# Sums of w2 in a fused attention and FFN kernel: places of their own in the first half's chunks, GpSimd additions beside the queries

## The chip, the cores and the metric

The kernel runs on one core of a Trainium2 chip. The metric is the device time in microseconds (us) of one execution; lower is better. In the text TensorE is the engine that the profile calls PE (PEld its weight loads), VectorE is DVE, ScalarE is ACT, GpSimd is POOL, and SP is the engine that issues most DMAs.

## The reference

One block: layer norm, linear attention with 32 heads of 18, and a gated FFN, on 2048 rows of 576 features, all in float32.

```python
phi = lambda t: jnp.where(t > 0, t + 1, jnp.exp(t)) + 1e-6
pq, pk = phi(q), phi(k)
kv = jnp.einsum("bhsd,bhse->bhde", pk, v);  z = jnp.einsum("bhsd->bhd", pk)
o = einsum("bhqd,bhde->bhqe", pq, kv) / (einsum("bhqd,bhd->bhq", pq, z) + 1e-6)
s = merge_heads(o) @ wo
h = gelu(xn @ w1 + b1)          # 4608 columns
g = silu(h @ w2 + b2)
out = x + s * g
```

## The kernel before

**Arithmetic.** Every product is made of float32r matmuls: each operand is split into a high part (a cast on ScalarE, `hi`) and a low part (a subtraction, mostly on VectorE, `lo`), and three products of parts are added. Around that stands a Strassen scheme: a 2x2 block product takes seven products, numbered 1 to 7, whose operands 4 to 7 are sums and differences of blocks. So w1, w2 and the activations need sums before they are split. For w2 these sums are blocks added to blocks. The function `add_to` makes such a sum with a DMA that accumulates into its destination; GpSimd issues it (line 497 in the profile), and may wait for one before issuing the next.

**Stages.** (1) Keys, values and the state, in pairs of row tiles. (2) Query rounds r = 0 to 9, one pair of tiles each (the class `Proj` for the projection, `Attend` for the attention product with kw = state x wo). A round has 14 steps; steps 0 to 6 stand behind the seven products of the projection (in the order 1, 6, 7, 5, 2, 4, 3; their PSUM banks are a, b, z, e), steps 7 to 12 beside the two attention products (ps_s) and the transposes of the next pair's scaled queries (ptp, source pbuf, split into th and tl). Beside the queries, w2's sums 5 and 6 for chunks 4 to 8 are formed, split (w2o) and stored to DRAM. (3) The FFN in two halves of the rows, each going through nine chunks of w2. A chunk has 28 steps: 14 behind the products of two up blocks (`Up`, banks a, b, zy, e), then 14 behind the two halves of the seven down products (`product`, pm, in the order 1, 2, 7, 4, 5, 3, 6), whose results VectorE adds to macc. Steps 7 to 15 form the activations' sums (`HOps.S`, GpSimd), and their splits are h_h and h_l. In the first half, each chunk also loads the next chunk's w2, forms its sums 7 and 4, and forms and splits the next w1 blocks (`W1.T` on GpSimd, tiles w1t and w1raw; `hi` and `lo` give wa, wb, w).

**What sets the order.** The whole order is written by hand: `add(step, function, ...)` appends to a table, and `at_step(step)` issues what stands there once TensorE's part of the step has been issued. Each engine works through its instructions strictly in that order, so one that waits holds everything behind it. `plan_w1` puts the work on a w1 block into the table by two tables of steps, P1 (the second block of a chunk) and P0 (the first block of the next chunk).

**Sums 7 and 4 of a chunk.** Product 7's operand is B(0,1) + the block at (1,1); it is accumulated into the raw tile w2raw. Product 4's has a tile of its own, w2t4: it is loaded, the block (1,0) is accumulated into it, and at last the finished sum 7 (`sum4`, part 1). The tile pool `fr` also has the tags w2t5 and w2t6, which only the tail uses.

Of the kernel before, what the change touches and what calls it, by code (L numbers as in the profile page):

```python
# [8 lines left out]
F32 = mybir.dt.float32  # L9
# [6 lines left out]
P = 128  # L16
S = 2048
D = 576
HD = 288
# [7 lines left out]
CF = 4  # L27
NC = NF // CF
# [9 lines left out]
NSP = 14  # L38
# [4 lines left out]
def linear_attention_gated_ffn(ctx, tc, x, wqkv, wo, w1, b1, w2, b2, out):  # L43
    nc = tc.nc
    SUB, MUL, ADD = ALU.subtract, ALU.mult, ALU.add
# [426 lines left out]
    w2raw, w2op = {}, {}  # L472

    def w2_blocks(c):
        return w2[c].rearrange("p (r n a d) -> p r n a d", r=2, n=2, a=2)
# [15 lines left out]
    def w2_block(c, i):  # L491

        r, n = {5: (0, 0), 6: (1, 1), 4: (1, 0)}[i]
        return w2raw[c][r][:, n]

    def add_to(dst, src):
        nc.gpsimd.dma_start(dst, src, accum_op=ADD)

    def w2_sum(j):
        c, i = SUMS[j]  # L500
        add_to(w2_block(c, i), {5: w2_blocks(c)[:, 0, 1], 6: w2_block(c, 5), 4: w2_block(c, 6)}[i])

    def w2_hi(j):
# [13 lines left out]
    def add(step, fn, *args):  # L517
        plans.setdefault(step, []).append((fn, args))
# [195 lines left out]
    for p in range(1, NPAIR):  # L714
        plan_pair(p)
        base = p * NSP
# [36 lines left out]
    base = NPAIR * NSP  # L753
# [23 lines left out]
    kw_h = kwp.tile([P, KT, D], F32R, name="kw_h")  # L777
    kw_l = kwp.tile([P, KT, D], F32R, name="kw_l")
# [4 lines left out]

    krs = []

    def split_kw(k, elo):
        nc.scalar.copy(kw_h[:, k, :], krs[k])
        elo.tensor_tensor(kw_l[:, k, :], krs[k], kw_h[:, k, :].bitcast(F32), op=SUB)

    def fold_wo(hooks):  # L790

# [199 lines left out]
    for r in range(NPAIR + 2):  # L991
        base = (NPAIR + r) * NSP
        if r <= 5:
            for k, i in enumerate(RELOAD[r]):
                add(base + (9, 11, 12)[k], x_reload, i)
        if r < NPAIR:
            a, b = q_tiles(r)
        if 2 <= r <= NPAIR:
            late = 2 * (r == 2)
            add(base + late, den_mul, r - 1, 1)  # L1000
            for s in range(2):
                add(base + 2 + s + late, den_sum, r - 1, s)
                add(base + 2 + s + late, den_div, r - 1, s)
        if 1 <= r < NPAIR:
            add(base + (12 if r > 1 else 15), den_mul, r, 0)
            add(base + (4 if r != 2 else 5), pad, 0)
            add(base + (6 if r != 2 else 7), pad, 1)
            if r > 1:
                add(base + 9, p_hi, r - 1, 0)
                add(base + 9, p_lo, r - 1, 0)  # L1010
            add(base + NSP, p_hi, r - 1, 1)
            add(base + NSP + 1, p_lo, r - 1, 1)
        if 1 <= r < NPAIR:
            a, b = q_tiles(r)
            at = base + 2 * (r == 2)
            add(at + 7, phi_exp, a, e_bufs[0])
            add(at + 7, phi_exp, b, e_bufs[1])
            add(at + 7, phi_max, a, e_bufs[0])
            add(at + 8, phi_max, b, e_bufs[1])
            add(at + (8 if r > 1 else 14), phi_add, a)  # L1020
            add(at + (9 if r > 1 else 15), phi_add, b)
        if r == 1:
            add(base + NSP + 2, split_kw, 2, nc.vector)
            add(base + NSP + 4, split_kw, 3, nc.vector)
        if 2 <= r <= 6:
            add(base, w2_load, r + 2, *((w1p, "wa") if r % 2 == 0 else (w2rp, "w2raw")))
        if r == 2:
            add(base + 8, w2_sum, 2 * r + 5)
        if 3 <= r <= 7:
            n = 2 * r + 3  # L1030
            add(base + 1, w2_sum, n + 1)
            if r < 7:
                add(base + 8, w2_sum, n + 2)
            for j in range(2):
                add(base + 7 + j, w2_hi, n + j)
                add(base + 9 + j, w2_lo, n + j)
        if r == 0:
            phi_exp(a, e_bufs[0]), phi_exp(b, e_bufs[1])
            fold_wo({
                0: [lambda: phi_max(a, e_bufs[0]), lambda: phi_max(b, e_bufs[1])],  # L1040
                1: [lambda: phi_add(a), lambda: phi_add(b), lambda: den_mul(0, 0), lambda: den_mul(0, 1)],
            })
            split_kw(0, nc.vector)
            den_all(0, 0)
            add(base + NSP + 2, den_all, 0, 1)
            add(base + NSP + 3, split_kw, 1, nc.vector)
        elif r < NPAIR:
            pr = Proj(Q_ORDER[r], wkq, q_tiles(r), mu2)
            for k, i in enumerate(K_UP):
                pr.step(i)  # L1050
                if (r, k) == (2, 0):
                    transpose_p(0, 1)
                if (r, k) == (1, 5):
                    transpose_p(0, 0), p_hi(0, 0), p_lo(0, 0)
                at_step(base + k)
        if 1 <= r < NPAIR:
            for s in range(2):
                at = Attend(r - 2, s) if r >= 2 else None
                for k in range(2):
                    if at:  # L1060
                        at.part(7 * k, 7 * k + 7)
                    at_step(base + 7 + 3 * s + k)
                if at:
                    at.store()
                    transpose_p(r - 1, s)
                at_step(base + 9 + 3 * s)
            if r == 7:
                w1t[0], w1t[1] = W1(0), W1(1)
                w2_raw0.append(load_w2_raw(0))
        if r == 0:  # L1070
            for k in range(9, 14):
                at_step(base + k)
        elif r == NPAIR:
            w = w1t[0]
# [12 lines left out]
            p_hi(r - 1, 0), p_lo(r - 1, 0)  # L1087
            pad(1)
            w.hi("a"), w.lo("a")
            w.T(4)  # L1090
            at.part(7, 14)
            at.store()
            transpose_p(r - 1, 1)
            p_hi(r - 1, 1), p_lo(r - 1, 1)
        elif r > NPAIR:
            for s in range(2):
                at = Attend(r - 2, s)
                at.part(0, 14)
                at.store()
                if s == 0:  # L1100
                    for j in (6, 7, 5):
                        w.hi(j), w.lo(j)
                else:
                    for j in ("b", 4):
                        w.hi(j), w.lo(j)
# [8 lines left out]
    fr = ctx.enter_context(tc.tile_pool(name="fr", bufs=1, side="right", reuse_waits="tile"))  # L1114
# [67 lines left out]
    class W2:  # L1182


        def __init__(self, n):
            self.n, self.ops, self.tiles = n, {}, {}

        def load_raw(self):
            self.raw = raw = load_w2_raw(self.n) if self.n else w2_raw0[0]
            self.B = lambda r, n: raw[:, r, n]  # L1190
            self.src = {1: self.B(0, 0), 2: self.B(1, 0), 3: self.B(1, 1), 7: self.B(0, 1)}
            if 0 < self.n < NC:
                self.src[4] = fr.tile([P, CF // 2, HD], F32, tag="w2t4", name=f"w2t4_{self.n}", bufs=1)
                nc.sync.dma_start(self.src[4], w2_blocks(self.n)[:, 0, 0])

        def sum7(self):
            add_to(self.src[7], w2_blocks(self.n)[:, 1, 1])
# [235 lines left out]
    def plan_w1(add, w, base, T, hi, lo):  # L1433
# [8 lines left out]
    )  # L1442
    P0 = dict(
        T={5: 24, 6: 24, 7: 25, 4: 25},
        hi={"a": 14, 6: 25, 7: 26, 5: 26, "b": 27, 4: 27},
        lo={"a": 14, 6: 25, 7: 26, 5: 26, "b": 27, 4: 27},
    )


# [19 lines left out]
    w2t = {}  # L1469
# [5 lines left out]
    for step in range(n_chunks):  # L1475
# [4 lines left out]
        if half == 0:  # L1480
            plan_w1(add, w1t[2 * step + 1], base, **P1)
            w2c = w2t[step]
            if not step:
                add(base + 2, w2c.sum7)
            for i, at in (PW2 if step else PW2_FIRST).items():
                add(base + at, w2c.hi, i)
                add(base + at, w2c.lo, i)
            if step == 0:
                for i, at in W2_SUMS_FIRST.items():
                    add(at, w2t[0].load, i)  # L1490
        if half == 0 and c < NC - 1:
# [2 lines left out]
            add(base + 13, lambda n=2 * step + 2: plan_w1(add, w1t[n], base, **P0))  # L1494
            make(W2, w2t, step + 1)
            nxt = w2t[step + 1]
            add(base + (8 if step else 10), nxt.load_raw)
            add(base + (16 if step else 17), nxt.sum7)
            add(base + (16 if step else 17), nxt.sum4, 0)
            add(base + 21, nxt.hi, 2)  # L1500
            add(base + 21, nxt.lo, 2)
            add(base + (21 if step else 22), nxt.sum4, 1)
            add(base + 27, nxt.hi, 4)
            add(base + 27, nxt.lo, 4)
            for i, at in W2_SUMS_NEXT.items():
# [103 lines left out]
```

## Time and profile before

| | us |
|---|---|
| median of 3 runs (1120.41 to 1122.63) | 1121.7 |
| the profiled execution | 1122.14 |
| its span, first to last instruction | 1120.4 |
| TensorE busy | 1098.9 |
| VectorE busy | 810.8 |
| ScalarE busy | 505.4 |
| GpSimd busy | 459.5 |
| mean granted TensorE clock | 0.996 |

An instruction's row has its start in the span, its duration, engine, line, operation and output<-inputs; in brackets stand the engine's idle time before it and what ended it. A row of waits has the total, the number and the longest. Buffer numbers are left out of most names, so several tiles can share one. The query rounds 2 to 7 lie between 180 and 275 us, the first half's chunks between 291 and 709.

### The profile page before, as it was taken

How to read it: one execution, taken by the hardware profiler on the slowest of the kernel's cores; microseconds unless marked ns; L12 is line 12 of the kernel's file. 1: busy time of each engine (PE TensorE's matmuls, PEld its weight loads, DVE VectorE, ACT ScalarE, POOL GpSimd, SP SyncE). 2: the span in 40 equal slices, each digit the busy share in tenths (PEclk: the TensorE clock that was granted, in tenths of full speed). 3: DMA queues.
4: the chain of work that ended last, by engine and by line, in shares of the span. 5: the costliest groups of instructions: out<-in, count | busy, mean ns of one | idle time of the engine just before them, and what ended most of it. 6: DMA issues, size and time to landing. Idle time of an engine off the chain costs nothing.

```text
span 1120.4 us, 18755 instructions
## 1 busy us (share of the span) xinstructions
PE 1098.9 (98%) x6924; PEld 1017.2 (91%) x6924; DVE 810.8 (72%) x1242; ACT 505.4 (45%) x913; POOL 459.5 (41%) x419
## 2 busy tenths in 40 slices
PE   8999999999999999999999999999999999999997
PEld 7899998999898998988989889899898998988987
DVE  6877666656598888988889888666475574664756
ACT  6766554535545454454544544524233242242352
POOL 5854433344354444544545434324224132242340
PEclk9999999999999999999999999999999999999999
DMA  5887747895998679687796879977666666766243
GB/s 202 299 265 275 257 129 216 275 293 197 349 313 336 198 267 316 190 333 225 246 320 180 318 208 373 369 263 261 216 200 225 206 203 210 230 198 223 87 135 120
DMA packets 95818, 272.50 MB, mean 243 GB/s; under 512 B 10413, under 2 KB 21165, under 8 KB 93679
## 3 DMA queue, kind: packets, MB, share of 16 engines
q1 hardware_dynamic: 89391, 258.32, 65.2%
q0 software_dynamic: 6336, 12.98, 7.4%
q8 instruction: 55, 0.90, 0.3%
q14 instruction: 36, 0.29, 0.1%
HBM read 165.05 MB, written 100.01 MB: 237 GB/s over the span
## 4 chain that ended last, share of the span: by engine, by line
PE 90%; DVE 4%; ACT 3%; DMA 1%; issue 1%; POOL 1%; DVEq 0%; POOLq 0%; ACTq 0%
PE pm L1279 32%; PE e L1141 12%; PE a L1141 10%; PE zy L1141 10%; PE ps_s L885 5%; PE pl L411 5%; PE b L1141 4%; PE e L356 2%; PE z L356 2%; PE a L356 2%; PE pd L1402 2%; DVE h_l L915 1%; PE ps_kva L464 1%; DMA kr<-kw 1%; PE b L356 1%
## 5 line engine op out<-in xcount | busy, mean ns | idle before, releaser
L912 ACT CAST h_h<-g 128x512 fp32r<-128x512 f32 x204 | 120.1, 621 | 140.6 <-PE pm L1279 139.5
L915 DVE TENSOR_TENSOR h_l<-g,h_h 128x512 fp32r<-128x512 f32 x204 | 169.3, 830 | 0.0
L1287 DVE TENSOR_TENSOR macc<-macc,pm 128x576 f32<-128x576 f32 x128 | 96.1, 751 | 36.8 <-PE pm L1279 36.7
L1246 POOL TENSOR_TENSOR mid<-g 128x512 f32<-128x512 f32 x34 | 44.0, 1294 | 184.7 <-ACT g L1149 184.7
L1141 PE MATMUL a<-xH,wa 128*128 128x512 f32 x360 | 117.1, 390 | 0.0
L1289 DVE TENSOR_TENSOR macc<-pm,macc 128x576 f32<-128x576 f32 x90 | 68.0, 755 | 18.4 <-PE pm L1279 17.6
L1149 ACT ACTIVATE g<-b,b1c 128x512 f32<-128x512 f32 x36 | 24.8, 688 | 124.5 <-DVE b L1167 124.5
L1141 PEld LDWEIGHTS a<-xH,wa 128*128 128x128 f32 x360 | 67.6, 188 | 13.7
L1141 PE MATMUL e<-xSH,wb 128*128 128x512 f32 x216 | 66.6, 390 | 0.2 <-DVE b L1167 0.2
L1240 POOL TENSOR_TENSOR g<-g 128x512 f32<-128x512 f32 x34 | 49.5, 1456 | 22.3 <-DVE h_l L915 20.9
L1158 ACT COPY mid<-a 128x512 f32<-128x512 f32 x36 | 21.2, 588 | 83.0 <-PE a L1141 82.6
L1141 PE MATMUL a<-xL,wa 128*128 128x512 f32 x144 | 56.2, 391 | 0.0
L1373 POOL TENSOR_TENSOR fin1l<-fin1h,fin1l 128x288 f32<-128x288 f32 x8 | 6.4, 806 | 120.0 <-DMA fin1l<-s_dram 61.6
L1243 POOL TENSOR_TENSOR g<-g 128x512 f32<-128x512 f32 x34 | 49.9, 1467 | 13.1 <-DVE h_l L915 11.8
L1237 POOL TENSOR_TENSOR g<-g 128x512 f32<-128x512 f32 x34 | 50.9, 1496 | 2.7
L1161 DVE TENSOR_TENSOR mid<-b,mid 128x512 f32<-128x512 f32 x36 | 24.7, 685 | 37.5 <-PE b L1141 37.4
L1141 PE MATMUL b<-xSH,w 128*128 128x512 f32 x144 | 50.2, 389 | 0.0
L1141 PE MATMUL zy<-xSH,w 128*128 128x512 f32 x144 | 50.2, 389 | 0.0
L1141 PE MATMUL e<-xSH,w 128*128 128x512 f32 x144 | 50.2, 389 | 0.0
L1141 PE MATMUL zy<-xH,w 128*128 128x512 f32 x144 | 50.2, 389 | 0.0
L1141 PEld LDWEIGHTS e<-xSH,wb 128*128 128x128 f32 x216 | 40.5, 188 | 9.1 <-DVE b L1167 0.6
L915 DVE TENSOR_TENSOR h_l<-mid,h_h 128x512 fp32r<-128x512 f32 x34 | 42.4, 1248 | 6.6 <-ACT h_h L912 6.6
(930 smaller groups left out, 3570.1 us busy)
## 6 DMA issues: line engine op xcount, KB each, us to landing
op<-w SPq DMA_DIRECT2D x72, 256.0 KB
w<-op SPq DMA_DIRECT2D x72, 256.0 KB
w1raw<-w SPq DMA_DIRECT2D x18, 640.0 KB
w2raw<-w SPq DMA_DIRECT2D x10, 1152.0 KB
op_a<-wa SPq DMA_DIRECT2D x18, 640.0 KB
wa<-op_a SPq DMA_DIRECT2D x18, 640.0 KB
op<-w2o SPq DMA_DIRECT2D x19, 576.0 KB
w2r<-w SPq DMA_DIRECT2D x6, 1152.0 KB
```

The lines of the kernel that those rows point to most:

```text
L356: nc.tensor.matmul(ps, st, mv, start=first and n == 0, stop=n == len(seq) - 1, skip_group_check=True,)
L411: nc.tensor.matmul(self.ps[n], st, self.wk(hl, k, n), start=(i == 0), stop=(i == n_all - 1))
L885: nc.tensor.matmul(self.ps[h], st[:, k, :], w[:, k, h * HD : (h + 1) * HD], start=(i == 0), stop=(i == len(self.seq) - 1),)
L912: nc.scalar.copy(pair[0], src)
L915: eng.tensor_tensor(pair[1], src, pair[0].bitcast(F32), op=SUB)
L1141: nc.tensor.matmul(ps.rearrange("p (c j) -> p c j", c=4), st, mv, start=first and n == 0, stop=n == len(seq) - 1, skip_group_check=True,)
L1237: tt(src[5, pr], A(1, 1), A(1, 0), op=SUB)
L1240: tt(src[6, pr], src[5, pr], A(0, 0), op=ADD)
L1243: tt(src[3, pr], src[6, pr], A(0, 1), op=SUB)
L1279: nc.tensor.matmul(ps[:, q, :HD], hs[p][st][:, cs], m[:, p, :], start=(n == 0 and i not in CHAIN), stop=(n == len(seq) - 1), skip_group_ch ...
L1287: nc.vector.tensor_tensor(dst, dst, src, op=SUB)
L1289: nc.vector.tensor_tensor(dst, src, dst, op=ADD)
```

## The change

It has three parts.

Round 2 of the queries splits two rows of kw. Where one step did the cast and the subtraction of row 2 (`split_kw`), and a later one those of row 3, the casts now stand in steps 2 and 3 and the subtractions in steps 3 and 4. At DVE, around the row that reads bank e after product 5 (`rt<-e`); `kr` are raw rows, `den` softmax denominators. Before:

```order
L788 TENSOR_TENSOR kw_l<-kr_2073,kw_h 128x576
L364 SCALAR_TENSOR_TENSOR rt<-e_2199,scr 128x288
L788 TENSOR_TENSOR kw_l<-kr_2082,kw_h 128x576
L829 TENSOR_REDUCE den_2262<-e_2040 128x32
L832 TENSOR_SCALAR den_2262<-den_2262 128x32
```

The same place now:

```order
L364 SCALAR_TENSOR_TENSOR rt<-e_2199,scr 128x288
L794 TENSOR_TENSOR kw_l<-kr_2073,kw_h 128x576
L794 TENSOR_TENSOR kw_l<-kr_2082,kw_h 128x576
L838 TENSOR_REDUCE den_2262<-e_2040 128x32
L841 TENSOR_SCALAR den_2262<-den_2262 128x32
```

`rt<-e` has moved ahead of both subtractions.

Beside queries, rounds 3 to 7 form w2's sums with `tensor_tensor` on GpSimd in place of an accumulating DMA. Both sums of a chunk stand in steps 4 and 5 of one round, where the DMAs stood in step 8 of the round before and in step 1; the casts (w2o) move from steps 7 and 8 to 9 and 11, the subtractions from 9 and 10 to 10 and 12. GpSimd from round 4 to round 5; `pbuf` are the scaled queries, L823 (now L832) multiplies for the denominators, w2r is chunk 5's and 6's raw w2. Before:

```order
L497 DMA w2r_2403<-w2r_2403 128x576
L836 TENSOR_TENSOR pbuf_2038<-scr,den_2612 128x576
L836 TENSOR_TENSOR pbuf_2039<-scr,den_2626 128x576
L497 DMA w2r_2591<-w 128x576
L823 TENSOR_TENSOR e_2040<-rt,zb 128x576
L823 TENSOR_TENSOR scr<-rt,zb 128x576
L497 DMA w2r_2592<-w2r_2591 128x576
L836 TENSOR_TENSOR pbuf_2038<-rt,den_2800 128x576
```

The same place now:

```order
L845 TENSOR_TENSOR pbuf_2038<-scr,den_2610 128x576
L845 TENSOR_TENSOR pbuf_2039<-scr,den_2624 128x576
L503 TENSOR_TENSOR w2r_2402<-w2r_2402 128x576 x2
L832 TENSOR_TENSOR e_2040<-rt,zb 128x576
L832 TENSOR_TENSOR scr<-rt,zb 128x576
L845 TENSOR_TENSOR pbuf_2038<-rt,den_2798 128x576
L845 TENSOR_TENSOR pbuf_2039<-rt,den_2812 128x576
L503 TENSOR_TENSOR w2r_2590<-w2r_2590 128x576
```

No DMA stands ahead of `pbuf` any more; two additions stand behind it.

In the first half's chunks, sums 4 and 7 of the next chunk get the tiles w2t5 and w2t6 (named w2s), loaded in steps 0 and 5 by a DMA each. The accumulation into sum 4 moves from step 16 to 12, that into sum 7 stays in 16 (17 in chunk 0 before), and sum 7 is added to sum 4 in 21 as before (22 in chunk 0 before). The raw load no longer serves sum 7. GpSimd in chunk 3, from the last operations on activations (g, mid) to the first on w1. Before:

```order
L1246 TENSOR_TENSOR mid<-g 128x512
L1237 TENSOR_TENSOR g<-g 128x512
L1240 TENSOR_TENSOR g<-g 128x512
L1243 TENSOR_TENSOR g<-g 128x512
L497 DMA w2raw_5228<-w 128x576
L497 DMA w2t_4_5230<-w 128x576
L497 DMA w2t_4_5230<-w2raw_5228 128x576
L937 TENSOR_TENSOR w1t_5506<-w1raw_5103 128x256
```

The same place now:

```order
L497 DMA w2s_4_5111<-w 128x576
L1254 TENSOR_TENSOR mid<-g 128x512
L1245 TENSOR_TENSOR g<-g 128x512
L1248 TENSOR_TENSOR g<-g 128x512
L1251 TENSOR_TENSOR g<-g 128x512
L497 DMA w2s_4_5198<-w 128x576
L497 DMA w2s_4_5111<-w2s_4_5198 128x576
L946 TENSOR_TENSOR w1t_5509<-w1raw_5109 128x256
```

One of the two accumulations that stood between the activations and the last one has moved ahead of the activations. Table P0 also moves the split of the next w1 block's part a (wa) from step 14 to step 24, on ScalarE, VectorE and, for its store, SP.

```diff
+        if here:
+            dst, b = w2_block(c, i), w2raw[c][0][:, 1] if i == 5 else w2_block(c, 5)
+            nc.gpsimd.tensor_tensor(dst, dst, b, op=ADD)
+            return
...
+    def kw_hi(k):
+        nc.scalar.copy(kw_h[:, k, :], krs[k])
+
+    def kw_lo(k, elo):
+        elo.tensor_tensor(kw_l[:, k, :], krs[k], kw_h[:, k, :].bitcast(F32), op=SUB)
...
-            add(base + NSP + 2, split_kw, 2, nc.vector)
-            add(base + NSP + 4, split_kw, 3, nc.vector)
+            for k, at_hi, at_lo in ((2, NSP + 2, NSP + 3), (3, NSP + 3, NSP + 4)):
+                add(base + at_hi, kw_hi, k)
+                add(base + at_lo, kw_lo, k, nc.vector)
...
-        if r == 2:
-            add(base + 8, w2_sum, 2 * r + 5)
         if 3 <= r <= 7:
             n = 2 * r + 3
-            add(base + 1, w2_sum, n + 1)
-            if r < 7:
-                add(base + 8, w2_sum, n + 2)
             for j in range(2):
-                add(base + 7 + j, w2_hi, n + j)
-                add(base + 9 + j, w2_lo, n + j)
+                add(base + (4, 5)[j], w2_sum, n + j, True)
+                add(base + (9, 11)[j], w2_hi, n + j)
+                add(base + (10, 12)[j], w2_lo, n + j)
...
-            if 0 < self.n < NC:
-                self.src[4] = fr.tile([P, CF // 2, HD], F32, tag="w2t4", name=f"w2t4_{self.n}", bufs=1)
-                nc.sync.dma_start(self.src[4], w2_blocks(self.n)[:, 0, 0])
+        def load_sum(self, i):
+            n = self.n
+            self.src[i] = fr.tile([P, 2, HD], F32, tag=f"w2t{5 + i // 7}", name=f"w2s{i}_{n}", bufs=1)
+            nc.sync.dma_start(self.src[i], w2_blocks(n)[:, 0, i // 7])
...
-        hi={"a": 14, 6: 25, 7: 26, 5: 26, "b": 27, 4: 27},
+        hi={"a": 24, 6: 25, 7: 26, 5: 26, "b": 27, 4: 27},
...
+            add(base + 0, nxt.load_sum, 4)
+            add(base + 12, nxt.sum4, 0)
+            add(base + 5, nxt.load_sum, 7)
+            add(base + 16, nxt.sum7)
             add(base + (8 if step else 10), nxt.load_raw)
-            add(base + (16 if step else 17), nxt.sum7)
-            add(base + (16 if step else 17), nxt.sum4, 0)
-            add(base + (21 if step else 22), nxt.sum4, 1)
+            add(base + 21, nxt.sum4, 1)
```

More of the change, by code (lines that the diff above doesn't have):

```diff
@@ L497, in add_to, with w2_sum @@
         nc.gpsimd.dma_start(dst, src, accum_op=ADD)
-    def w2_sum(j):
+    def w2_sum(j, here=False):
         c, i = SUMS[j]
+        if here:
+            dst, b = w2_block(c, i), w2raw[c][0][:, 1] if i == 5 else w2_block(c, 5)
+            nc.gpsimd.tensor_tensor(dst, dst, b, op=ADD)
+            return
         add_to(w2_block(c, i), {5: w2_blocks(c)[:, 0, 1], 6: w2_block(c, 5), 4: w2_block(c, 6)}[i])
@@ L784, in linear_attention_gated_ffn @@
     krs = []
+    def kw_hi(k):
+        nc.scalar.copy(kw_h[:, k, :], krs[k])
+    def kw_lo(k, elo):
+        elo.tensor_tensor(kw_l[:, k, :], krs[k], kw_h[:, k, :].bitcast(F32), op=SUB)
     def split_kw(k, elo):
-        nc.scalar.copy(kw_h[:, k, :], krs[k])
-        elo.tensor_tensor(kw_l[:, k, :], krs[k], kw_h[:, k, :].bitcast(F32), op=SUB)
+        kw_hi(k), kw_lo(k, elo)
     def fold_wo(hooks):
@@ L1185, in __init__ @@
         def __init__(self, n):
-            self.n, self.ops, self.tiles = n, {}, {}
+            self.n, self.ops, self.tiles, self.src = n, {}, {}, {}
         def load_raw(self):
@@ L1190, in load_raw @@
             self.B = lambda r, n: raw[:, r, n]
-            self.src = {1: self.B(0, 0), 2: self.B(1, 0), 3: self.B(1, 1), 7: self.B(0, 1)}
-            if 0 < self.n < NC:
-                self.src[4] = fr.tile([P, CF // 2, HD], F32, tag="w2t4", name=f"w2t4_{self.n}", bufs=1)
-                nc.sync.dma_start(self.src[4], w2_blocks(self.n)[:, 0, 0])
+            self.src |= {1: self.B(0, 0), 2: self.B(1, 0), 3: self.B(1, 1)}
+        def load_sum(self, i):
+            n = self.n
+            self.src[i] = fr.tile([P, 2, HD], F32, tag=f"w2t{5 + i // 7}", name=f"w2s{i}_{n}", bufs=1)
+            nc.sync.dma_start(self.src[i], w2_blocks(n)[:, 0, i // 7])
         def sum7(self):
@@ L1444, in linear_attention_gated_ffn @@
         T={5: 24, 6: 24, 7: 25, 4: 25},
-        hi={"a": 14, 6: 25, 7: 26, 5: 26, "b": 27, 4: 27},
-        lo={"a": 14, 6: 25, 7: 26, 5: 26, "b": 27, 4: 27},
+        hi={"a": 24, 6: 25, 7: 26, 5: 26, "b": 27, 4: 27},
+        lo={"a": 24, 6: 25, 7: 26, 5: 26, "b": 27, 4: 27},
     )
@@ L1483, in linear_attention_gated_ffn @@
             if not step:
+                w2c.src[7] = w2c.B(0, 1)
                 add(base + 2, w2c.sum7)
```

## The prediction

> **What bounds the kernel now.** I read the page first (its engines' busy time), then TensorE's waits, the windows by round and by chunk, the chain of waits, and last the timelines of the engines around each gap.
>
> ```profile
> PE 1098.9 (98%) x6924; PEld 1017.2 (91%) x6924; DVE 810.8 (72%) x1242; ACT 505.4 (45%) x913; POOL 459.5 (41%) x419
> ```
>
> ```profile
> PE pm L1279 <- DVE h_l L915: 4.9, 7, 0.8
> PE ptp L853 <- DVE th L865: 2.3, 1, 2.3
> PE e L356 <- DVE rt L364: 1.5, 1, 1.5
> ```
>
> TensorE is busy for 98% of the span, so the change can win only TensorE's gaps and the slow matmuls behind them. The waits name three kinds: seven before a down product (pm), and one each in two query rounds. The windows (span, then busy time of PE, PEld, DVE, ACT, POOL, then clock and DMA) price each kind by pitch; a query round is 15.17 us long when nothing disturbs it.
>
> ```profile
> 180.00:195.02 15.02, 13.44 (x90) 12.97 (x89) 9.21 (x17) 6.89 (x15) 6.63 (x6) 0.89 0.63 203
> 195.02:210.19 15.17, 15.17 (x118) 15.17 (x118) 9.13 (x18) 8.10 (x18) 8.92 (x8) 1.00 0.80 227
> ...
> 225.37:243.64 18.27, 15.92 (x117) 15.72 (x117) 9.07 (x18) 7.76 (x17) 10.53 (x9) 0.95 0.92 287
> 243.64:259.63 15.99, 15.99 (x118) 15.99 (x118) 10.34 (x20) 7.64 (x16) 6.99 (x6) 0.95 0.89 273
> ...
> 340.55:386.56 46.01, 45.44 (x269) 41.20 (x269) 40.18 (x56) 22.02 (x41) 21.94 (x19) 1.00 0.74 254
> ...
> 617.39:663.58 46.19, 45.45 (x270) 41.21 (x269) 40.37 (x56) 22.04 (x41) 21.96 (x19) 1.00 0.74 250
> 663.58:708.68 45.10, 45.10 (x269) 41.15 (x269) 36.60 (x50) 21.41 (x34) 16.06 (x11) 1.00 0.98 371
> ```
>
> Rounds 5 and 6 lose 3.10 + 0.82 = 3.92 us; round 6 has no idle time, only the lower clock. Chunks 1 to 7 of the first half (340.55 to 663.58) take 323.03 us against 7 x 45.10 = 315.70 for a clean one: 7.33 us lost, 1.05 each. Chunk 0 loses nothing.
>
> **Part 1: round 2, the split of wo's rows.** TensorE's timeline and the chain of waits, then DVE, then POOL:
>
> ```profile
> 183.63 0.40 PE L356 MATMUL e<-wkq_h,xSH 128*128 128x288 f32 x1 [1.53 <-DVE rt L364]
> ```
>
> ```profile
> 183.63 2.08 PE e L356 x8
> 185.71 4.49 PE ps_s L885 x28
> 190.75 3.73 PE ps_s L885 x28
> ...
> 200.58 1.06 PE e L356 x8
> ```
>
> ```profile
> 181.33 1.87 DVE L788 TENSOR_TENSOR kw_l<-kr,kw_h 128x576 fp32r<-128x576 f32 x1 [0.62 <-ACT kw_h L787]
> 183.13 0.45 DVE L364 SCALAR_TENSOR_TENSOR rt<-e,scr 128x288 f32<-128x288 f32 x1
> 183.50 0.74 DVE L788 TENSOR_TENSOR kw_l<-kr,kw_h 128x576 fp32r<-128x576 f32 x1
> ```
>
> ```profile
> 181.18 1.41 POOL L823 TENSOR_TENSOR scr<-scr,zb 128x576 f32<-128x576 f32 x1
> 185.68 1.17 POOL L836 TENSOR_TENSOR pbuf<-scr,den 128x576 f32<-128x576 f32 x1 [3.09 <-DVE den L833]
> ```
>
> Product 3 adds into the bank e that rt<-e must have read. That read stood on DVE behind a kw_l which first waited for a cast (0.62) and then ran 1.87 us instead of 0.74, ending 0.6 after the GpSimd multiply it met. TensorE lost 1.53 idle, and at the lower clock 2.08 - 1.06 = 1.02 on e and 4.49 - 3.73 = 0.76 on ps_s: 3.3 us. The change puts rt<-e ahead of both kw_l. The copy of bank a moves behind the second cast on ACT; its bank isn't needed again before the second attention product, 4 us on. Late next: the softmax denominators behind both kw_l. They come only 0.4 earlier (rt<-e is gone from their front), so the first pbuf ends near 186.5 and its pad near 186.8, while TensorE wants to transpose it at 182.1 + 1.06 + 3.73 = 186.9. I leave 0 to 0.5 of new stall: gain 2.8 to 3.4, taken 3.2.
>
> **Part 2: beside the queries, additions for accumulating DMAs.** POOL in round 5, then round 3's undisturbed rows:
>
> ```profile
> 233.15 0.88 POOL L497 DMA_DIRECT2D w2r<-w2r  x1 [4.18 <-DMA w2r<-w]
> ```
>
> ```profile
> 201.78 1.17 POOL L836 TENSOR_TENSOR pbuf<-rt,den 128x576 f32<-128x576 f32 x1 [0.60 <-PE e L356]
> 203.94 0.76 DVE L445 SCALAR_TENSOR_TENSOR scr<-e,scr 128x576 f32<-128x576 f32 x1 [1.66 <-ACT e L442]
> 208.54 0.29 DVE L865 TENSOR_TENSOR th<-ptp,th 64x128 fp32r<-64x128 f32 x1
> 209.65 0.55 PE ptp L853 x5
> ```
>
> In round 5 POOL waited 4.18 us for the first sum before it could issue the second, and pbuf stood behind it. Pads, exponentials, two w2o casts and the th cast then ran late on ACT, and TensorE waited 2.35 us for th. The change takes the ten accumulating DMAs (0.88 of POOL each) out and adds ten additions, two per round in rounds 3 to 7, behind pbuf, with operands loaded a round earlier; the casts go behind th. No addition is in the trace before. Nearest is POOL's 128x576 multiply, 1.41 alone; bounds 1.17 (pbuf, the same size with a broadcast operand) and 1.9 (1.41 plus a wait for a DVE operation). Two cost 2.8 us, from 203.0 to 205.8 in round 3. They lie beside phi_max (L445), which I let wait its whole 1.41 twice: the second ends near 207. ACT's th cast waits for the first phi_max but no longer for the two casts, so th is ready near 208.2 against TensorE's 209.65: hidden, with 1.4 to spare. If that cover is gone, a round loses what round 5 lost, up to 3.9. Gain 3.92, less 0.1 for what these neighbours may still cost: 3.8.
>
> **Part 3: first half's chunks.** POOL, DVE and the chain in chunk 3, then the DMA issues (median from issue to landing last):
>
> ```profile
> 459.29 0.88 POOL L497 DMA_DIRECT2D w2raw<-w  x1
> 466.56 0.87 POOL L497 DMA_DIRECT2D w2t<-w2raw  x1 [5.48 <-DMA w2t<-w]
> 467.12 1.07 POOL L937 TENSOR_TENSOR w1t<-w1raw 128x256 f32<-128x256 f32 x1
> 469.32 0.73 POOL L942 TENSOR_TENSOR w1raw<-w1raw 128x256 f32<-128x256 f32 x1
> ```
>
> ```profile
> 453.57 1.21 DVE L915 TENSOR_TENSOR wa<-w1raw,wa 128x640 fp32r<-128x640 f32 x1
> 464.84 0.75 DVE L915 TENSOR_TENSOR w__5445<-w2raw,w__5445 128x576 fp32r<-128x576 f32 x1
> 465.51 0.68 DVE L915 TENSOR_TENSOR h_l<-g,h_h 128x512 fp32r<-128x512 f32 x1
> 466.78 1.98 DVE L915 TENSOR_TENSOR h_l<-g,h_h 128x512 fp32r<-128x512 f32 x1
> 473.25 0.75 DVE L1287 TENSOR_TENSOR macc<-macc,pm 128x576 f32<-128x576 f32 x1 [0.51 <-PE pm L1279]
> 480.94 0.69 DVE L1167 TENSOR_TENSOR b<-e,mid 128x512 f32<-128x512 f32 x1
> ```
>
> ```profile
> 451.26 12.88 PE pm L1279 x96
> 468.81 6.00 PE pm L1279 x43
> 482.57 1.59 PE e L1141 x7
> ```
>
> ```profile
> w2raw<-w POOLq DMA_DIRECT2D x9, 288.0 KB, 4.5
> ```
>
> POOL may issue the last accumulation only when the second has landed, at 466.56; the four w1t/w1raw operations of the next W1 follow at once and meet the h_l at 466.78, which takes 1.98 instead of 0.68. The 96 matmuls of four products take 12.88 us, 3.2 each, so the sixth product (number 3) could start at 467.3; it needs this h_l 0.67 later, at its sixth matmul, and gets it at 468.81. In chunk 0 the last accumulation is issued a step later and meets nothing; that chunk is the evidence that the collision, not the DMA, costs the time. The change puts the first accumulation four steps earlier, into POOL's idle time (cost nothing: 0.88 before the next S operation, and if that idle time were gone each S would be 0.9 later). One sum is left at the old place. It starts some 0.4 earlier, because the 1.21 us wa no longer meets the S operations: 458.9 + 4.5 + 0.3 = 463.7 instead of 466.56. The three w1t/w1raw operations, 0.73 each when nothing blocks them, so run from 464.6 on, against the 0.75, 0.68 and second h_l of DVE's row. I alternate them, one waiting for the other: 464.6, 465.3 (w), 465.8, 466.5 (h_l), 467.0 (macc beside the last). The macc then ends near 467.8; product 3's bank needs it at 467.3 and the second h_l ends near 468.3. So about 0.5 us of the 1.05 stays. Ends: if the sum lands 0.5 earlier nothing stays; if 0.5 later, 1.1 stays. Chunk 0, clean now, gets the same collision: 8 x 0.55 = 4.4 remain of 7.33, gain 2.9 (from -1.5 to 7.3).
>
> The wa split goes to step 24, behind the last h_l: 0.75 (as much as the 576 columns of w__5445) to 1.21 us of DVE, in a stretch where DVE waited for TensorE (the 0.51 at 473.25 is one of three such waits, 1.07 in all). So I cost it at nothing. If that cover is gone, b<-e,mid of the next up block is late: it ended at 481.6 and TensorE's e, which reuses its bank, began at 482.6, so 0.9 us are left before TensorE waits, in each chunk. The last of the four POOL operations writes what wa reads and now waits for it, until about 470; behind it on POOL stands only the next W1's first operation. On SP wa's 640 KB store moves with it, past one load of w2. SP issues one more 288 KB load per chunk, twelve steps ahead of its use, in stretches with DMA busy 0.74.
>
> **The sum.** 3.2 + 3.8 + 2.9 = 9.9 us off the profiled execution's 1122.1 (span 1120.4 and 1.7 around it): 1112.2. The median of the runs, 1121.7, is 0.4 below that execution: 1111.8.
>
> In the Trainium skill, "TensorE: Matmul & The Clock Gate", section "What's actually happening", the clock falls after an idle window of about 3.4 us. By that alone neither query gap would cost clock, the two would return 1.53 + 2.35, and the sum would be 6.8. The trace disagrees: after 1.53 us of idle time the e product took 2.08 instead of 1.06.
>
> **Rivals.** A: the w1t operations collide as before, only 2 us sooner. For it: macc and h_l stand in the same DVE order, and a landing 0.5 later is enough. Gain 7.0 - 1 = 6: 1115.7. B: the sum lands early enough and the chunks run at 45.10: gain 14.3: 1107.4; for it, the landing sum no longer shares its time with a second one. C, slower: the additions hold phi_max and the next multiplies up until th misses TensorE in every round. It decides where they cost over 2.8 + 1.4 us per round. At 3.9 in four more rounds, and the old 3.9 kept, 1121.7 - 6.1 + 15.6 = 1131. For it: kw_l's 1.87 beside a GpSimd operation; against it: 1.4 us of slack. The Trainium skill, "SBUF — State Buffer", section "Who interferes with whom", says the later of a vector operation with two SBUF inputs and a GpSimd operation that reads SBUF is fully blocked; the trace agrees at kw_l, and by it a phi_max waits at most one addition. D: other waits stand right behind the removed ones and nothing moves: 1121.7.
>
> **How the numbers follow.** Forecast 0.48, A 0.22, B 0.12, C 0.11, D 0.07. A measurement of this kernel tells 0.2% (2.2 us) from no change. Faster is forecast, A and B: 0.82; same 0.07; slower 0.11. The range reaches from B to A with the ends of parts 1 and 2: 1106 to 1117.
>
> **What would show it.** Right: no wait of e L356 and none of ptp on th; clock 1.00 in rounds 2 and 5; POOL waiting for no DMA beside the queries; chunk pitch near 45.6, 0 included. Wrong: pitch at 46.1 (A) or 45.1 (B); th waits in rounds 3 to 7 (C); waits for kr<-kw or pbuf in place of e's (D).

## The result

| | kernel before | changed kernel |
|---|---|---|
| median of 18 runs, us | 1120.08 | 1117.7 |
| lowest and highest run, us | 1116.43 to 1123.05 | 1116.7 to 1119.52 |
| ratio of the times, 95% interval | 1 | 0.998 (0.9971 to 0.9988) |
| profiled execution, us | 1122.14 | 1118.17 |

The change gains 2.4 us of the 9.9 that were forecast; 1117.7 lies above the range's end of 1117. The two profiled executions differ by 4.0 us, more than the medians, and the runs of the kernel before spread over 6.6 us, those of the changed one over 2.8.

The page of the changed kernel, first the busy times, then TensorE's waits:

```profile
PE 1095.4 (98%) x6924; PEld 1014.2 (91%) x6924; DVE 812.6 (73%) x1242; ACT 504.2 (45%) x913; POOL 466.1 (42%) x419
```

```profile
PE pm L1287 <- DVE macc L1295: 6.4, 7, 1.1
...
PE pm L1287 <- ACT h_h L921: 0.7, 1, 0.7
...
PE a L1147 <- DMA xH<-x_dram: 0.5, 1, 0.5
```

Both waits in the queries are gone, and their slow clock with them. In the chunks the waits for `h_l` (4.9 us) are gone, but waits for `macc`, which must read a bank before the next product writes it, came in their place with 7.1 us, counting the one put down to a cast. The windows by stage (up to the first chunk; chunk 0; 1 to 7; 8; the rest) of the kernel before and of the changed one:

```profile
0.00:295.39 295.39, 284.82 (x2095) 276.62 (x2096) 197.50 (x398) 168.12 (x324) 144.12 (x155) 0.99 0.75 247
295.39:340.55 45.16, 45.16 (x270) 41.15 (x269) 38.78 (x57) 23.28 (x43) 21.56 (x20) 1.00 0.95 314
340.55:663.58 323.03, 318.14 (x1877) 288.46 (x1877) 282.28 (x386) 154.30 (x287) 153.73 (x133) 1.00 0.77 259
663.58:708.68 45.10, 45.10 (x269) 41.15 (x269) 36.60 (x50) 21.41 (x34) 16.06 (x11) 1.00 0.98 371
708.68:1120.40 411.72, 405.67 (x2418) 369.86 (x2417) 255.59 (x355) 138.28 (x227) 124.03 (x101) 1.00 0.63 206
```

```profile
0.00:288.73 288.73, 281.78 (x2095) 273.73 (x2096) 206.52 (x398) 168.66 (x324) 153.74 (x155) 1.00 0.72 242
288.73:335.03 46.30, 45.33 (x269) 41.17 (x269) 39.02 (x57) 23.03 (x43) 21.81 (x20) 1.00 0.90 303
335.03:658.39 323.36, 317.30 (x1877) 288.23 (x1877) 275.12 (x386) 152.88 (x287) 150.54 (x133) 1.00 0.77 266
658.39:704.24 45.85, 45.35 (x269) 41.19 (x269) 37.33 (x51) 21.53 (x34) 16.03 (x11) 1.00 0.96 362
704.24:1116.40 412.16, 405.67 (x2418) 369.86 (x2417) 254.60 (x354) 138.09 (x227) 123.96 (x101) 1.00 0.63 207
```

Up to the first chunk 6.66 us are gained; chunk 0 gives back 1.14, chunks 1 to 7 another 0.33, chunk 8 0.75 and the rest 0.44. Chunk 3 shows how (it starts at 427.43, where it was 432.68 before, so 5.25 earlier); POOL, then DVE:

```profile
458.73 0.86 POOL L497 DMA_DIRECT2D w2s<-w2s  x1 [4.28 <-DMA w2s<-w]
459.30 1.06 POOL L946 TENSOR_TENSOR w1t<-w1raw 128x256 f32<-128x256 f32 x1
460.44 1.15 POOL L948 TENSOR_TENSOR w1t<-w1raw,w1t 128x256 f32<-128x256 f32 x1
461.55 1.17 POOL L951 TENSOR_TENSOR w1raw<-w1raw 128x256 f32<-128x256 f32 x1
466.45 0.74 POOL L954 TENSOR_TENSOR w1raw<-w1raw,w1t 128x256 f32<-128x256 f32 x1 [3.73 <-DVE wa L924]
```

```profile
459.51 1.48 DVE L924 TENSOR_TENSOR w__5448<-w2raw,w__5448 128x576 fp32r<-128x576 f32 x1
460.91 1.22 DVE L924 TENSOR_TENSOR h_l<-g,h_h 128x512 fp32r<-128x512 f32 x1
462.06 0.74 DVE L1295 TENSOR_TENSOR macc<-macc,pm 128x576 f32<-128x576 f32 x1
462.72 0.68 DVE L924 TENSOR_TENSOR h_l<-g,h_h 128x512 fp32r<-128x512 f32 x1
```

```profile
462.94 0.51 PE L1287 MATMUL pm<-w__5211,h_h 128*128 128x288 f32 x2 [0.95 <-DVE macc L1295]
```

The sum is released at 458.73, which is 463.98 on the clock of the kernel before (463.7 was forecast). The three w1 operations follow. The split of w2 meets the first and takes 1.48 in place of 0.75, the `h_l` behind it 1.22 in place of 0.68, so the `macc` behind both ends at 462.80; TensorE waits 0.95 us for it, and the chunk lasts 46.28 against a clean 45.10.

### The profile page after: what moved, and what is told of

Same layout as the page of the kernel before. It is cut to its first block, busy times and chain, and to the rows that moved or that the text cites. A ratio compares the mean times of both kernels' runs of the same rounds, so it can differ in the third digit from the quotient of the medians.

```text
span 1116.4 us, 18757 instructions
## 1 busy us (share of the span) xinstructions
PE 1095.4 (98%) x6924; PEld 1014.2 (91%) x6924; DVE 812.6 (73%) x1242; ACT 504.2 (45%) x913; POOL 466.1 (42%) x419
## 4 chain that ended last, share of the span: by engine, by line
PE 88%; DVE 4%; DMA 3%; ACT 2%; issue 1%; POOL 1%; SPq 0%; DVEq 0%; POOLq 0%; ACTq 0%
PE pm L1287 30%; PE e L1147 12%; PE a L1147 10%; PE zy L1147 10%; PE pl L411 5%; PE ps_s L894 5%; PE b L1147 4%; PE e L356 2%; DMA xH<-x_dram 2%; PE a L356 2%; PE z L356 2%; PE pd L1410 2%; PE ps_kva L464 1%; PE b L356 1%; DVE h_l L924 1%
## 5 line engine op out<-in xcount | busy, mean ns | idle before, releaser
L924 DVE TENSOR_TENSOR h_l<-g,h_h 128x512 fp32r<-128x512 f32 x204 | 159.5, 782 | 0.0
L1248 POOL TENSOR_TENSOR g<-g 128x512 f32<-128x512 f32 x34 | 49.5, 1456 | 22.2 <-DVE h_l L924 20.9
L1251 POOL TENSOR_TENSOR g<-g 128x512 f32<-128x512 f32 x34 | 49.9, 1467 | 13.1 <-DVE h_l L924 11.8
L1245 POOL TENSOR_TENSOR g<-g 128x512 f32<-128x512 f32 x34 | 47.1, 1386 | 2.7
L1155 ACT ACTIVATE g<-e,b1c 128x512 f32<-128x512 f32 x36 | 24.8, 688 | 49.2 <-DVE e L1180 49.2
```

Of the source, the lines that this page charges most:

```text
L924: eng.tensor_tensor(pair[1], src, pair[0].bitcast(F32), op=SUB)
L1155: nc.scalar.activation(g, ps, AF.Gelu_apprx_tanh, bias=b1c[:, f : f + 1])
L1248: tt(src[6, pr], src[5, pr], A(0, 0), op=ADD)
L1251: tt(src[3, pr], src[6, pr], A(0, 1), op=SUB)
```

## Experiments

Times are medians, beside the median of the kernel before from the same runs; these lie between 1119.5 and 1120.9, so differences between kernels of different experiments are good to about 1 us. A pitch is the difference of two chunk starts in the trace (a chunk is counted from its first e product); a chunk of some 46 us is called stalled, one of some 45.1 clean. An operation is held where its row is longer than the same operation's undisturbed one. L946 to L954 are the four operations of `W1.T`.

**The query parts alone.** The kernel before with parts 1 and 2 of the change and none of part 3.

> The kernel before with the change's query parts alone (order of kw's split; additions in place of accumulating DMAs); the chunks are untouched. Theory 1, the two stalls of the profiled execution stand in every execution of the kernel before: all of the 6.7 us that the trace shows up to the first chunk is gained in every run, so 1120.1 - 6.7 = 1113.4, ratio 0.994; pitch of chunk 0 45.1, of 1 to 7 46.1. Theory 2, these stalls hang on when DMAs land and come and go between executions (the runs of the kernel before span 6.6 us, those of the changed one 2.8): the profile looks as in theory 1, but the median gains only 3 to 5 us, ratio 0.9955 to 0.997, and the spread of this kernel's runs is as small as that of the changed one.

Measured: 1113.71 beside 1119.54, ratio 0.9943 (0.9928 to 0.9959): 5.8 us, between the two theories' sizes; in the trace the stretch from the first e product to the first chunk is 6.56 shorter, and the runs spread over only 2.6 us, as the second theory had it. But the pitches were not those that either theory gave: 46.34, 46.16, 46.13, 46.25 in chunks 1 to 4 and 45.18, 45.18, 45.19 in 5 to 7. The same chunk code stalls in some chunks and not in others. Two of its chunks side by side, chunk 4 (stalled) and chunk 5 (clean), POOL and DVE of each:

```profile
508.62 0.87 POOL L497 DMA_DIRECT2D w2t<-w2raw  x1 [5.46 <-DMA w2t<-w]
509.18 1.07 POOL L946 TENSOR_TENSOR w1t<-w1raw 128x256 f32<-128x256 f32 x1
```

```profile
508.84 1.97 DVE L924 TENSOR_TENSOR h_l<-g,h_h 128x512 fp32r<-128x512 f32 x1
```

```profile
554.97 0.88 POOL L497 DMA_DIRECT2D w2t<-w2raw  x1 [5.57 <-DMA w2t<-w]
555.53 1.08 POOL L946 TENSOR_TENSOR w1t<-w1raw 128x256 f32<-128x256 f32 x1
```

```profile
555.09 0.69 DVE L924 TENSOR_TENSOR h_l<-g,h_h 128x512 fp32r<-128x512 f32 x1
```

Where `h_l` starts 0.34 ahead of the row of the w1 operation it is held for 1.3 us; where it starts 0.44 ahead it isn't held at all. A landing that is a tenth of a microsecond later decides over 1.05 us of the chunk.

**The chunk part alone.**

The changed kernel, with `w2_sum`, `split_kw` and their steps as in the kernel before.

> The changed kernel with the queries of the kernel before: the change's chunk part alone (places of their own for sums 4 and 7, their steps, wa's split at 24). Theory 1, the chunk part as such loses what the trace shows (1.14 in chunk 0, 0.33 in 1 to 7, 0.75 in chunk 8): 2.2 us slower than before, ratio 1.002; pitch 46.3 in chunk 0, 46.2 in 1 to 7, 45.85 in chunk 8. Rival, the loss comes from where the queries end now: pitch 45.5 or below in some chunks and a time 2 to 3 us below the kernel before.

Measured: 1124.74 beside 1119.54, ratio 1.0039 (1.0025 to 1.0054); pitches 45.92 to 46.44 in all of chunks 0 to 7, 45.10 in chunk 8. The chunk part is a loss by itself, and of 5.2 us, not 2.2. The 2.2 was a difference to one profiled execution of the kernel before, with seven chunks stalled and 2.6 us over the median beside which this run stands; how many chunks stall in its other runs was not recorded. All eight of this kernel's chunks, 0 to 7, stall. Chunk 8 is clean here.

**w2's split out of the tight product.**

```diff
-            add(base + 21, nxt.lo, 2)
+            add(base + 25, nxt.lo, 2)
```

The tight product is the fifth of the seven (number 5): VectorE's work beside it fills its time, and TensorE waits behind it.

> The changed kernel with the subtraction that splits w2's block 2 (w<-w2raw, 0.75 us on VectorE) in step 25 instead of 21, out of the product in which GpSimd's w1t operations meet VectorE. Theory (VectorE's queue in that product is too full: two h_l, two macc and this split, held twice by GpSimd): the h_l behind it waits for one GpSimd operation (about 0.7) and nothing else is late, so the bank is read in time: pitch 45.1 to 45.4 in chunks 0 to 7, 6 to 9 us less than the changed kernel: 1109 to 1112. Rival (the wait for the bank comes from a cast, or from GpSimd's hold on h_l alone): pitch stays at 46.0 to 46.3, 1117.7.

Measured: 1114.43 beside 1119.54, ratio 0.9941 (0.9924 to 0.9957), 3.3 us below the changed kernel; pitches 45.36 to 45.60. The waits for the bank are gone and by the pitches the split was worth some 0.7 of the 1.15 us per chunk, 5.7 in eight. The median shows less: in the profiled execution, 1114.39, the first e product comes 2.5 us later than in the changed kernel's (see the last section), and two of the six runs lie at 1111.9 and 1112.1. The forecast of 45.1 to 45.4 was a little too good: both `h_l` of this product still take 1.27 instead of 0.68 beside GpSimd.

**wa's split back in step 14.**

```diff
-        hi={"a": 24, ...   lo={"a": 24, ...
+        hi={"a": 14, ...   lo={"a": 14, ...
```

> The changed kernel with the split of wa back in step 14 from 24. Theory (moving wa's split moved its 640 KB store by some 10 us, the store is missing from the quiet stretch and lands in the one where DMA is full, so x's loads of chunk 8 land too late): chunk 8 back to 45.1, 0.75 us gained there. In chunks 0 to 7 wa's 1.21 us stand beside the S operations again, the sum lands 0.4 later and w2's split gets through ahead of the first GpSimd operation: one hold less, pitch 45.5 to 46.1: in all 1110 to 1117. Rival (chunk 8's wait comes from the extra load of w2 per chunk): chunk 8 stays at 45.85. Rival for the pitch: 46.2 as in the changed kernel.

Measured: 1123.68 beside 1119.54, ratio 1.0041 (1.0026 to 1.0057): 6 us slower than the changed kernel, outside every case stated. Pitches 45.96 in chunk 0 and 46.96 to 47.25 in 1 to 7. In its chunk 3, POOL and DVE:

```profile
463.82 1.17 POOL L951 TENSOR_TENSOR w1raw<-w1raw 128x256 f32<-128x256 f32 x1
464.96 0.72 POOL L954 TENSOR_TENSOR w1raw<-w1raw,w1t 128x256 f32<-128x256 f32 x1
```

```profile
461.40 1.87 DVE L924 TENSOR_TENSOR w__5453<-w2raw,w__5453 128x576 fp32r<-128x576 f32 x1
463.19 1.22 DVE L924 TENSOR_TENSOR h_l<-g,h_h 128x512 fp32r<-128x512 f32 x1
464.33 0.74 DVE L1295 TENSOR_TENSOR macc<-macc,pm 128x576 f32<-128x576 f32 x1
464.99 1.24 DVE L924 TENSOR_TENSOR h_l<-g,h_h 128x512 fp32r<-128x512 f32 x1
```

With wa split early nothing holds the fourth w1 operation back; it follows the third, and VectorE is held three times where it was held twice. Not all of the chunk's 0.93 us over the changed kernel's come from the third hold: the first is longer too (1.87 where it was 1.48), and TensorE waits 1.33 for `macc` where it waited 0.95, before it waits another 0.17 for the third `h_l`. Moving wa's split to 24 is the one piece of part 3 that gained. Chunk 8 came to 45.25.

**The w1 operations early.**

```diff
-        T={5: 24, 6: 24, 7: 25, 4: 25},
+        T={5: 6, 6: 6, 7: 6, 4: 25},
...
-            add(base + 13, lambda n=2 * step + 2: plan_w1(add, w1t[n], base, **P0))
+            add(base + 5, lambda n=2 * step + 2: plan_w1(add, w1t[n], base, **P0))
```

> The changed kernel with three of the four GpSimd operations on the next w1 block (w1t, w1t, w1raw) in step 6 of the chunk, ahead of the activations' sums, instead of 24 and 25; only the fourth stays behind the last accumulation, where it waits for wa. Theory (they and nothing else hold VectorE when the sum lands): pitch 45.1 to 45.3 in chunks 0 to 7; GpSimd was idle for some 8 us ahead of the activations' sums, so these start at most 1 us later, hidden; 8 to 9 us less than the changed kernel: 1108 to 1110. Rival 1 (the issue of the accumulation itself is enough): pitch 45.5 to 46. Rival 2 (the wait moves to the activations' sums): h_l late in the up blocks, pitch over 45.5 with waits before the first products.

Measured: 1109.16 beside 1120.94, ratio 0.9901 (0.9883 to 0.9918), 8.5 us below the changed kernel. The windows (chunk 0; 1 to 7; 8):

```profile
289.19:334.76 45.57, 45.44 (x270) 41.08 (x269) 38.63 (x57) 22.94 (x43) 21.39 (x20) 1.00 0.92 304
334.76:650.46 315.70, 315.70 (x1877) 288.10 (x1877) 262.63 (x386) 152.89 (x287) 152.30 (x133) 1.00 0.79 272
650.46:695.53 45.07, 45.07 (x269) 41.16 (x269) 36.55 (x50) 21.40 (x34) 16.07 (x11) 1.00 0.98 369
```

Seven chunks at exactly 45.10, TensorE without idle time. So the three operations behind the landing were the whole stall of chunks 1 to 7; chunk 0 still loses 0.47. The activations' sums, which now stand behind them, made nothing late there that TensorE waits for.

**The same without places of their own.** Query parts, the chunks of the kernel before, w1 operations in 6 and wa's split in 24.

> The query parts alone, with the chunks of the kernel before (sum 4 and 7 in a row, no places of their own), the same three GpSimd operations in step 6 and wa's split in 24. Theory (the three operations are the cost, not where sum 7 and 4 have their places): pitch 45.1 to 45.3, 1108 to 1110, the same as the run with own places and these operations early. Rival (two sums in a row cost by themselves): pitch 45.5 to 46.1 in the chunks whose last accumulation is issued 33.6 to 33.9 us after the chunk's start.

Measured: 1108.22 beside 1120.94, ratio 0.9895 (0.9876 to 0.9914): the lowest time here, 0.9 below the run with places of their own, 0.44 of it in chunk 0. Chunk 0 takes 45.13, 8 takes 45.10; 1 to 7 together:

```profile
333.88:649.58 315.70, 315.70 (x1878) 288.08 (x1877) 267.75 (x386) 152.82 (x287) 151.57 (x133) 1.00 0.79 266
```

The two sums in a row cost nothing once nothing follows them: the places of their own, the core of part 3, gain nothing. In chunk 2, POOL and DVE:

```profile
412.60 0.89 POOL L497 DMA_DIRECT2D w2t<-w2raw  x1 [5.64 <-DMA w2t<-w]
```

```profile
413.00 0.68 DVE L924 TENSOR_TENSOR h_l<-g,h_h 128x512 fp32r<-128x512 f32 x1
```

An `h_l` that starts in the middle of the issue of the accumulation runs undisturbed. So the issue doesn't hold it; the operation behind it does, where one follows at once (see "The fourth w1 operation let go").

**The order of kw's split alone.** Part 1 of the change on the kernel before.

> The kernel before with the split of wo's rows in the new order, and nothing else. By the prediction 3.2 us less (2.8 to 3.4): 1116.3 beside 1119.5, ratio 0.997; in the trace no wait of e for rt in round 2, round 5's wait for th still there. Rival (the softmax denominators come late in place of e): 1 to 2 us less.

Measured: 1119.49 beside 1120.94, ratio 0.9989 (0.9976 to 1.0003): no gain that can be told. In its trace round 2's wait of e for rt is gone as forecast, but the queries as a whole are only 0.41 us shorter (from the first e product, at 52.09, to the first chunk, at 295.06, against 52.01 and 295.39). TensorE's waits, then POOL in rounds 3 and 5:

```profile
PE ptp L858 <- DVE th L870: 3.7, 2, 3.0
```

```profile
204.72 0.90 POOL L497 DMA_DIRECT2D w2r<-w  x1 [4.16 <-DMA w2r<-w]
...
232.24 0.88 POOL L497 DMA_DIRECT2D w2r<-w2r  x1 [5.06 <-DMA w2r<-w]
```

A round that starts earlier waits longer for the accumulating DMAs. Ahead of round 5 GpSimd gets to the issue of one 1.78 us earlier than in the kernel before (223.44 against 225.22), but has what it waits for next only 0.91 earlier (232.24 against 233.15): a wait of 5.06 against 4.18. TensorE, which waited for th only in round 5, waits 0.70 in round 3 and 2.98 in round 5.

**The additions alone.** Part 2 of the change on the kernel before.

> The kernel before with GpSimd additions in place of the accumulating DMAs beside the queries, and nothing else. By the prediction 3.8 us less (3.5 to 3.9): 1115.7 beside 1119.5, ratio 0.9966; in the trace no wait of ptp for th, GpSimd's additions 1.2 to 1.9 us each, th's wait none in rounds 3 to 7, round 2's wait of e for rt still there. Rival C (additions hold phi_max): th late in each of rounds 3 to 7, slower than before.

Measured: 1114.88 beside 1120.94, ratio 0.9952 (0.9934 to 0.9969): 6 us by the medians, 3.5 to 7.4 by the interval. In the trace the queries are 3.83 us shorter (52.14 to 291.69), as forecast to 0.1; round 2 still waits 1.54 for rt. Part 1 on top of it (the query parts alone: 54.13 to 290.95) gains another 2.73 in the traces. The medians don't bear that out: 1114.88 here and 1113.71 with both parts differ by 1.2, about what such a comparison is good to, and the profiled execution here, 1118.05, is the slowest of six, 3.2 over their median.

**The accumulation into sum 7 two steps earlier.**

```diff
-            add(base + 16, nxt.sum7)
+            add(base + 14, nxt.sum7)
```

> The changed kernel with the accumulation into sum 7 in step 14 instead of 16, ahead of three of the activations' sums instead of behind all of them. It then lands before GpSimd is through with those, and the three w1 operations follow at once, some 4 us earlier than in the changed kernel: they meet the h_l of the products before the tight one. Theory (what counts is which product the operations fall into; the h_l there are ready 1.5 us and more ahead of their product): pitch 45.1 to 45.5 in chunks 0 to 7, 5 to 9 us less than the changed kernel: 1109 to 1113. Rival (VectorE has no slack in any product): the delay is carried on to the same wait, pitch 46 and more, 1117 or slower.

Measured: 1115.44 beside 1119.90, ratio 0.9951 (0.9936 to 0.9967). Pitches 45.77 to 45.81 in most chunks, 46.90 and 46.71 in chunks 0 and 5. Neither theory: 2.3 us below the changed kernel, but 0.7 per chunk stays. Chunk 3, set beside chunk 3 of the run without places of their own, a clean one, loses 0.41 of it two products before the place where the changed kernel waits, and 0.26 at that place. The rows suggest why, though no run tests it: the issue now stands ahead of three activations' sums, which run up to 0.8 us later, and the `macc` behind VectorE's work on them ends 0.8 later, just before TensorE goes on. VectorE carries part of the delay on to the place of the second loss.

**The fourth w1 operation let go.** The run without places of their own, wa's split back in 14.

> The run with the query parts, the chunks of the kernel before and three w1 operations in step 6, now with wa's split in step 14 as before: the fourth w1 operation doesn't wait for wa any more and follows the last accumulation at once. Theory (each operation that follows the landing holds VectorE once): one hold of 0.5 to 0.7 us per chunk where the landing meets an h_l, pitch 45.1 to 45.6, 0 to 4 us more than that run: 1108.2 to 1112. Rival (wa's 1.21 us beside the activations' sums are the greater cost): 45.6 and more, over 1112.

Measured: 1115.00 beside 1119.90, ratio 0.9958 (0.9935 to 0.9981), 6.8 us over the run that it changes (7 by the two ratios). Pitches 45.18 in chunks 0, 3 and 5 and 46.10 to 46.33 in the other five. One operation behind the landing costs as much as four did, 1.05 us: it is the first hold, of 1.26, that lies in the tight place. wa's 1.21 us beside the activations' sums are not the cost: they stand in the three clean chunks too. In chunk 2, POOL and DVE:

```profile
414.56 1.09 POOL L954 TENSOR_TENSOR w1raw<-w1raw,w1t 128x256 f32<-128x256 f32 x1
```

```profile
414.26 1.94 DVE L924 TENSOR_TENSOR h_l<-g,h_h 128x512 fp32r<-128x512 f32 x1
```

This `h_l` starts 0.27 us into the issue of the accumulation, at 413.99; one that started 0.40 into it ran undisturbed in the run before, where no operation followed. The size was missed: a hold is 1.26 where 0.5 to 0.7 was stated.

**The kernel before, a second execution.**

> The kernel before, unchanged, in a second profiled execution. Theory (its chunk stalls hang on whether the last accumulation's issue comes a tenth of a us ahead of an h_l or behind it): the stalled chunks are not the same seven; 3 to 7 of them at 46.0 to 46.3, the others at 45.1 to 45.3, and the time moves by 1.05 us for each. Rival (the stalls are the same in every execution): 1 to 7 at 46.0 to 46.3 again.

Measured: 1120.72. Chunk 5 is clean (45.19), 1 to 4, 6 and 7 stall. Counting all five traces with this chunk code (twice the kernel before, and the runs of part 1, part 2 and both), 7, 6, 5, 6 and 4 chunks stall. The query waits move as well: round 2's wait of e for rt, 1.53 in the first execution, is 0.2 here, and round 5's wait for th has grown from 2.35 to 4.17:

```profile
PE ptp L853 <- DVE th L865: 4.2, 1, 4.2
...
PE e L356 <- DVE rt L364: 0.2, 1, 0.2
```

**The changed kernel, a second execution.**

> The changed kernel, unchanged, in a second profiled execution. Theory (in the changed kernel the last sum lands where it always meets VectorE, while chunk 8's late load of x was chance): chunks 0 to 7 at 45.9 to 46.5 again, chunk 8 at 45.1 to 45.25, 1117.2 to 1118. Rival (wa's later store delays x's load each time): chunk 8 at 45.6 to 45.9 again.

Measured: 1117.81. Chunks 0 to 7 at 46.05 to 46.52, chunk 8 at 45.10. The changed kernel stalls in chunks 0 to 7 in both executions; chunk 8's 0.75 did not come back, and the reason stated for it, wa's later store, falls: the chunk part alone has that store too and a clean chunk 8.

## Why the prediction was wrong

**Part 1, 3.2 us: the wait went, the gain is not shown in full.** With the additions in place it gained 2.73 in the traces, without them 0.41; by the medians 1.2 with them and nothing that can be told without. The sum treated the two waits as independent. They are linked: round 2's wait stands ahead of the first accumulating DMA, and what an earlier round 2 does to the waits for these DMAs in rounds 3 and 5 was not asked. "Late next: the softmax denominators" named the wrong thing. It did no harm here since part 2 removes the DMAs. And 1.53 was read from one execution: in the second one this wait is 0.2, while th's is 4.17.

**Part 2, 3.8 us: right.** 3.83 in the trace, inside the interval of the medians; parts 1 and 2 together gain 5.8 of 7.0 by the medians. The additions take longer than forecast:

```profile
L503 POOL TENSOR_TENSOR w2r<-w2r 128x576 f32<-128x576 f32 x7 | 10.8, 1544 | 0.2
L503 POOL TENSOR_TENSOR w2r<-w2r,w2r 128x576 f32<-128x576 f32 x3 | 5.5, 1818 | 0.2
```

1.54 and 1.82 are inside the bounds of 1.17 to 1.9; two cost up to 3.4 instead of 2.8 and the slack of 1.4 bore it. Rival C did not happen.

**Part 3, 2.9 us gained: wrong, it lost 2.2 in the two traces** (1.14 + 0.33 + 0.75, the last not repeated), and 4 by the medians of the changed kernel and of the query parts alone; both lie below the stated end of -1.5. Three steps of it:

- "About 0.5 us of the 1.05 stays" was mis-sized: 1.18 stayed in chunk 3. The landing was forecast to 0.3 us, but I gave the w1 operations 0.73 each and let VectorE lose little where they alternate. Measured, w2's split loses 0.73, `h_l` 0.54, and the operations themselves take 1.06 to 1.17. That the split stands in the same product was in DVE's rows; I did not add up that product's own work there: two `h_l`, two `macc` and one split, 3.6 us by their durations and 3.2 by the distance of their starts, in a product of 3.2. No hold fits. Moving the split away brought the stall to 0.4, and putting the three w1 operations elsewhere ended it.
- "Chunk 0, clean now, gets the same collision" was right in kind: 1.14 there.
- The 7.33 us to be won were read from one execution as if every one lost them. Here seven of seven chunks stalled; in other traces four to six did. A lottery that is drawn at a tenth of a microsecond was turned into a certain loss. That the profiled executions differ by 4.0 us and the medians by 2.4 fits this, but is not shown to come from it. What of the 5.2 us that the chunk part alone loses in the medians goes beyond the 2 to 3 that the traces show is not settled; the two profiled executions of the kernel before lie over its median.

wa's split was costed at nothing. It was worth 6 us: the fourth operation's wait for it keeps that operation off VectorE (6.8 us in the run without places of their own). The prediction names that wait and asks only what harm it does.

**The case that came.** Rival A, the operations colliding as before only 2 us sooner, is what the trace shows, though the wait is now for `macc`, behind w2's split, and no longer for `h_l`; its 1115.7 lies 2 us below the time. It stood at 0.22 because I took an earlier landing for a better one without asking what work lies there.

**The base.** The median of 18 runs is 1.6 us below the one that the forecast started from. The gain was forecast too high by 7.5 us, and the base too high by 1.6: the forecast came out 5.9 too low.

## What to carry to other kernels

Add up a product's own work on the second engine before moving anything into or out of it: here a product whose work already equalled its time turned holds into a stall, and moving them by 2 us only chose another victim. Move the holder instead: three GpSimd operations put where GpSimd was idle gained 8.5 us, and no wait of TensorE came in their place in chunks 1 to 7. And before a stall in one trace is booked as a gain, look at whether the same code stalls each time it runs, in other executions as well as in the repeats of a loop.

## What the runs showed of the hardware

- GpSimd holds VectorE from before its own row. In the pairs above, an `h_l` that starts 0.34 us ahead of the GpSimd row is held and ends 0.56 us after that operation; one that starts 0.44 ahead is not held. So it is in all traces of this case, in the first half's chunks: 38 `h_l` that start 0.06 to 0.42 us ahead of the row take 1.69 to 2.05, nine that start 0.44 to 0.64 ahead take 0.68 or 0.69. The issue of the DMA just before is not the holder (0.68 us in the middle of an issue).
- VectorE operations with one operand in PSUM are untouched: `macc`, which reads `pm` in PSUM, takes 0.74 to 0.76 beside every one of these operations, in all traces. The Trainium skill, "SBUF — State Buffer", section "Who interferes with whom", says that a VectorE instruction contends where it has two SBUF inputs, not with one; the traces agree, with 1.97 for `h_l` and 0.74 for `macc`.
- The first 50 us differ between executions of the same code, and the granted clock with them. The changed kernel, then the run with w2's split moved, which has the same instructions there:

```profile
0.00:50.00 50.00, 44.46 (x311) 41.60 (x311) 34.25 (x75) 34.90 (x61) 33.71 (x46) 1.00 0.67 242
```

```profile
0.00:50.00 50.00, 43.97 (x295) 41.18 (x296) 33.21 (x72) 32.55 (x56) 32.40 (x45) 0.97 0.63 223
```

At 0.97 the first e product starts at 54.33 instead of 51.84. So 2.5 us of difference between two traces can lie ahead of anything that was changed; the stages were compared from there on.
